# Banded attention with top-1 experts on one core: a block's transposes of p in one run, 64-row transposes of x, one-hot rows first in a step, one ring of eight PSUM banks

## The chip, the cores and the metric

The kernel runs on one core of one Trainium2 chip. The metric is the device time of one execution in microseconds (us): the median of three runs before the change is 515.14 us (509.45 to 516.59). The profiled execution of the same kernel took 514.24 us, of which the profile's span covers 512.5 us.

## What is computed

Four batches of eight heads attend over 768 positions with 64 values each; a query sees 8 global keys and the 95 positions before it, with a slope per head for the distance. The 3072 rows of the result (512 wide) go through a gate that picks one of eight experts for each row; an expert takes the first 768 rows that chose it.

```python
scores = scale * np.matmul(q, k.transpose(0, 1, 3, 2))
scores = scores + bias[None, :, :, :]
scores = np.where(keep, scores, -1000000000.0)
a = np.exp(scores - np.max(scores, axis=-1, keepdims=True))
a = a / (np.sum(a, axis=-1, keepdims=True) + 1e-09)
x = np.matmul(a, v).transpose(0, 2, 1, 3).reshape(B * S, H * D)
...
logits = x @ w_gate
expert_idx = np.argmax(logits, axis=1)
probs = softmax(logits)
# row i is row pos[i] of its expert, as long as pos[i] < 768
h = np.maximum(np.einsum('ecd,edf->ecf', disp, w1), 0.0)
y = np.einsum('ecf,efd->ecd', h, w2)
out[i] = gate_w[i] * y[expert_idx[i], pos[i]]
```

## The kernel before, in words

**Stages.** Attention runs over 24 blocks of 128 rows (4 batches of 6 blocks) in a loop of 25 steps, t = 0 to 24. The experts' products follow; the change leaves them alone.

**One step.** A block has two units of four heads. Step t scores block t, finishes block t-1 and passes block t-2 on: `scores` (PE, L516, 16 matmuls a unit), `maxima` (DVE, L492, four a unit: adds the bias and takes the row's extreme), `exps` (ACT, L527, four a unit, which also give the row sums), `transpose_p` (PE L554, 16 transposes a unit into two banks, copied out by DVE L555 and ACT L556; a batch's first block has four transposes and one copy, L545 and L546), `weigh` (PE L575 and L578: x^T from p and v), `keep_x` (ACT L585: x^T out of PSUM), `sums` and `turn_sums` (POOL L531, DVE L536: one over the row sums) and `store_rows` (PE L165: four 128x128 transposes of x^T, DVE L168: scaled rows, then a store by SP).

**The gate.** Blocks go through the gate in groups of three, in steps of `route`: z (PE L186, ACT L189), l (PE L196, DVE L198 and L202), m (DVE L208 and L215, POOL L216 and L217), f (DVE L222 and L225 make `oh`, the one-hot rows; POOL L224 zeroes its last columns), n (PE L231 and L233 count with `oh`), p and s (slots), g (DVE L273) and the writes (POOL, three indirect DMAs to a table, L283). With b a group's last block, z stands in step b+2, l and m in b+3, f, n, p and s in b+4, and g with the writes in b+5. So steps repeat in threes: a z-step (t = 4, 7, 10, ...; the writes of the group before fall in it too), an l-step (5, 8, 11, ...) and an n-step (6, 9, 12, ...).

**What sets the order.** The order on PE, DVE, ACT and POOL is the order in which this loop is written; only SP's DMAs are scheduled. Transposes for a block's second unit stand in the middle of the next step, those for its first unit at the end of its own step (L554 for unit 2t). From t = 9 to 20 a step ends with a piece of the first experts' weights (ACT cast L137, POOL subtraction L138).

**PSUM.** Eight banks in three pools: four bankA (scores, x rows, l, n), two bankB (p transposed), two bankC (x^T and z).

Of the kernel before, what the change touches and what calls it, by code (L numbers as in the profile page):

```python
# [10 lines left out]
F32 = mybir.dt.float32  # L11
# [6 lines left out]
ALU = mybir.AluOpType  # L18
# [11 lines left out]
def fused(ctx: ExitStack, tc, q, k, v, wg, w1, w2, out, shape, n_global, n_local, cap):  # L30
# [19 lines left out]
    psA = ctx.enter_context(tc.tile_pool(name="psA", bufs=4, space=bass.MemoryType.PSUM))  # L50
    psB = ctx.enter_context(tc.tile_pool(name="psB", bufs=2, space=bass.MemoryType.PSUM))
    psC = ctx.enter_context(tc.tile_pool(name="psC", bufs=2, space=bass.MemoryType.PSUM))
# [5 lines left out]
    def bankA(shape, dt=F32):  # L58
        return psA.tile(shape, dt, name="bankA")

    def bankB(shape, dt=F32):
        return psB.tile(shape, dt, name="bankB")

    def bankC(shape, dt=F32):
        return psC.tile(shape, dt, name="bankC")
# [7 lines left out]
    warm_ps = bankB([P, DM])  # L73
# [76 lines left out]
    actx = ExitStack()  # L150
# [10 lines left out]
    def store_rows(i):  # L161
        xt = xts[i // 3]
        xr_ps = bankA([P, DM])
        for c in range(KC):
            nc.tensor.transpose(xr_ps[:, c * P:(c + 1) * P], xt[:, c, i % 3, :], ident)  # L165

        xr = rt.tile([P, DM], F32, name="xr_last", bufs=1) if i == NBLK - 1 else small.tile([P, DM], F32, name="xr")
        nc.vector.tensor_tensor(xr.rearrange("p (h d) -> p h d", h=H), xr_ps.rearrange("p (h d) -> p h d", h=H),  # L168
                                rss[i // 3][:, i % 3, :].unsqueeze(2).to_broadcast([P, H, D]), op=ALU.mult)
        nc.sync.dma_start(out=xrows[i * P:(i + 1) * P, :], in_=xr)  # L170
# [8 lines left out]
    def route_z(r):  # L179
        i0, T = r["i0"], r["T"]  # L180
        bank = bankC([P, 4 * P])
        r["bank"] = bankA if i0 + T < NBLK else lambda shape: bank[:, 2 * P:2 * P + shape[1]]
        z_ps = bank[:, 0:T * P]
# [158 lines left out]
    def turn_first(a):  # L342

        ps = bankA([P, KC, P])
# [69 lines left out]
    def banded():  # L414
# [81 lines left out]
        def scores(u):  # L496
# [9 lines left out]
            pss = un["ps"] = [bankA([P, 2, w]) for _ in range(2)]  # L506
# [31 lines left out]
        def transpose_p(u):  # L538
            un = units[u]
            j = blocks[u // 2][1]  # L540
            pt = un["pt"] = soft.tile([P, 2, 4, P], F32, name="pt", bufs=3)
            if j == 0:
                pb = bankB([P, 4, P])
# [4 lines left out]
            pbs = [bankB([P, 2, 4, HQ]) for _ in range(2)]  # L548
            for a in range(4):
                for part in range(2):  # L550
                    for n in range(2):
                        rows = slice(n * HQ, (n + 1) * HQ)
                        o = a * W + (1 - n) * HQ + part * (PREV + G)
                        nc.tensor.transpose(pbs[n][:, part, a, :], un["flat"][rows, o:o + P], ident[rows, rows])  # L554
            nc.vector.tensor_copy(pt[:, :, :, 0:HQ], pbs[0])  # L555
            nc.scalar.copy(pt[:, :, :, HQ:], pbs[1])  # L556

        def weigh(u):
# [4 lines left out]
            if half == 0:  # L563
                d["xt_ps"] = bankC([P, KC, P])
# [36 lines left out]
        for t in range(NBLK + 1):  # L601
# [3 lines left out]
            if t < NBLK:  # L605
                for u in (2 * t, 2 * t + 1):
                    scores(u)
                    maxima(u)
                exps(2 * t)
            route(t - 3, 1)  # L610
            if t < NBLK:
                route(t - 4, 3)
                route(t - 5, 7, 8)
            if t > 0:
                sums(t - 1)
                transpose_p(2 * t - 1)
            if t == NBLK - 1:
# [5 lines left out]
            if t > 1:  # L623
                store_rows(x)
# [9 lines left out]
            if t < NBLK:  # L634
                if t < NBLK - 1:
                    route(t - 3, 2)
                route(t - 4, 6)
                exps(2 * t + 1)
                transpose_p(2 * t)
# [20 lines left out]
    def dense():  # L660
# [7 lines left out]
        for i in range(NBLK):  # L668
            b, j = divmod(i, NB)
            if j == 0:  # L670
                kt = kv.tile([P, NP, S], F32, name="kt")
                vt = kv.tile([P, NB, H * D], F32, name="vt")
                for jj in range(NB):
# [5 lines left out]
                    ps = bankC([P, NP, P])  # L679
# [6 lines left out]
            ps = bankC([P, NP, P])  # L686
# [25 lines left out]
            for h in range(H):  # L712
                g, rows = h // 2, slice(64 * (h % 2), 64 * (h % 2) + 64)
                sc = dn.tile([P, S], F32, name="sc")
                for c0 in range(0, S, 384):
                    c = slice(c0, min(c0 + 384, S))
                    s_ps = bankA([P, c.stop - c0])
# [12 lines left out]
                x_ps = bankB([P, P])  # L730
                for jj in range(NB):
                    pt_ps = bankC([P, P])
# [32 lines left out]
    actx.close()  # L765

# [126 lines left out]
    h_ps = [bankB([P, T4]) for _ in range(FP)]  # L893
    y_ps = [bankA([P, DM]) for _ in range(FIXED)]
# [292 lines left out]
```

## Time and profile before

| | before |
|---|---|
| median of 3 runs | 515.14 us |
| profiled execution | 514.24 us |
| its span | 512.5 us |
| PE busy | 458.4 us (89%) |
| DVE, ACT, POOL busy | 285.4, 284.5, 126.0 us |
| start of step 2, of step 23 | 15.33, 154.42 us |

A row of a timeline gives the start, the length, the engine, the line and the tiles (out<-in), how many instructions it joins, and, in brackets, how long the engine had been idle before it and what ended that. PE counts as busy while a matmul is in flight, at whatever clock was granted.

### The profile page before, as it was taken

How to read it: one execution, taken by the hardware profiler on the slowest of the kernel's cores; microseconds unless marked ns; L12 is line 12 of the kernel's file. 1: busy time of each engine (PE TensorE's matmuls, PEld its weight loads, DVE VectorE, ACT ScalarE, POOL GpSimd, SP SyncE). 2: the span in 40 equal slices, each digit the busy share in tenths (PEclk: the TensorE clock that was granted, in tenths of full speed). 3: DMA queues.
4: the chain of work that ended last, by engine and by line, in shares of the span. 5: the costliest groups of instructions: out<-in, count | busy, mean ns of one | idle time of the engine just before them, and what ended most of it. 6: DMA issues, size and time to landing. Idle time of an engine off the chain costs nothing.

```text
span 512.5 us, 11225 instructions
## 1 busy us (share of the span) xinstructions
PE 458.4 (89%) x3914; PEld 377.2 (74%) x3914; DVE 285.4 (56%) x920; ACT 284.5 (56%) x790; POOL 126.0 (25%) x208
## 2 busy tenths in 40 slices
PE   8998788888887759999999999999999999999860
PEld 4776667666675548788888888897988888897640
DVE  6776766668775732645554556545555555546320
ACT  4987777788784303345546546546555455546330
POOL 6022143453433230423113113113113103003020
PEclk9999898999997987999999999999999999999995
DMA  8999659967622076754465365365455445241010
GB/s 258 308 331 295 120 126 299 209 200 176 114 94 79 24 182 224 237 187 155 117 198 174 118 219 171 106 206 170 133 184 185 112 161 172 66 128 68 5 41 12
DMA packets 51782, 81.53 MB, mean 159 GB/s; under 512 B 7689, under 2 KB 20009, under 8 KB 51660
## 3 DMA queue, kind: packets, MB, share of 16 engines
q1 hardware_dynamic: 45084, 65.00, 43.9%
q0 software_dynamic: 5888, 14.71, 9.2%
q8 instruction: 92, 1.51, 1.2%
q14 instruction: 30, 0.25, 0.2%
q10 hardware_dynamic: 688, 0.07, 0.1%
HBM read 67.10 MB, written 14.75 MB: 160 GB/s over the span
## 4 chain that ended last, share of the span: by engine, by line
issue 59%; PE 14%; POOL 13%; ACT 4%; DVE 3%; DMA 3%; another core or an unknown queue 1%; POOLq 0%; SPq 0%; ACTq 0%
POOL xg L352 5%; POOL out_dram L825 4%; PE bankB L554 3%; PE bankC L575 3%; PE bankA L516 2%; PE bankC L578 2%; POOL table L283 2%; DVE sc L492 2%; PE bankA L165 2%; ACT sc L527 2%; ACT pt L556 1%; DMA table<-pay,slot_of 1%; DMA K<-in_k_dram 1%; DMA w2r<-in_moe_w_dram 1%
## 5 line engine op out<-in xcount | busy, mean ns | idle before, releaser
L916 PE MATMUL bankB<-xh,w1h 128*128 128x416 f32 (+5 forms) x268 | 90.0, 341 | 3.0 <-DVE hl L964 1.8
L916 PE MATMUL bankB<-xh,w1l 128*128 128x416 f32 (+5 forms) x268 | 88.8, 337 | 0.8 <-issue 0.8
L963 ACT ACTIVATE hh<-bankB 128x512 fp32r<-128x512 f32 (+1 forms) x67 | 38.8, 580 | 90.3 <-PE bankB L916 81.9
L527 ACT ACTIVATE sc<-sc,mx 128x168 f32<-128x168 f32 (+1 forms) x192 | 80.0, 422 | 6.9 <-DVE mx L492 6.6
L964 DVE SCALAR_TENSOR_TENSOR hl<-bankB,hh 128x512 fp32r<-128x512 f32 (+1 forms) x67 | 44.6, 666 | 69.9 <-ACT hh L963 66.2
L924 PE MATMUL bankA<-w2h,hh 128*128 128x512 f32 x192 | 80.8, 421 | 2.0 <-issue 1.9
L925 PE MATMUL bankA<-w2l,hh 128*128 128x512 f32 x192 | 76.9, 401 | 0.0
L926 PE MATMUL bankA<-w2h,hl 128*128 128x512 f32 x192 | 76.8, 400 | 0.0
L916 PEld LDWEIGHTS bankB<-xh,w1h 128*128 128x128 f32 x268 | 50.6, 189 | 11.4 <-issue 6.0
L352 POOL DMA_INDIRECT xg<-xrows,gi x28 | 28.5, 1017 | 118.8 <-PE bankC L337 103.2
L916 PE MATMUL bankB<-xl,w1h 128*128 128x416 f32 (+5 forms) x268 | 57.3, 336 | 0.0
L916 PEld LDWEIGHTS bankB<-xh,w1l 128*128 128x128 f32 x268 | 50.6, 189 | 3.9 <-issue 1.1
L138 DVE TENSOR_TENSOR w1l<-wr,w1h 128x512 fp32r<-128x512 f32 x58 | 37.5, 689 | 27.8 <-ACT w1h L137 22.1
L966 ACT ACTIVATE hr<-bankB 128x256 f32<-128x256 f32 x64 | 24.6, 385 | 49.5 <-DVE hl L964 44.2
L492 DVE CUSTOM_DVE_ANT_0 sc<-bankA,bias 128x168 f32<-128x168 f32 (+1 forms) x192 | 49.2, 321 | 2.2 <-PE bankA L516 1.5
L138 DVE TENSOR_TENSOR w2l<-w2r,w2h 128x512 fp32r<-128x512 f32 x58 | 37.5, 688 | 19.2 <-ACT w2h L137 18.2
L916 PEld LDWEIGHTS bankB<-xl,w1h 128*128 128x128 f32 x268 | 47.0, 188 | 0.6
L924 PEld LDWEIGHTS bankA<-w2h,hh 128*128 128x128 f32 x192 | 36.7, 191 | 13.9 <-issue 7.6
L825 POOL DMA_INDIRECT out_dram<-ysb,to x16 | 15.9, 997 | 126.3 <-ACT ysb L817 123.9
L516 PE MATMUL bankA<-K,Q 64*64 64x168 f32 (+1 forms) x704 | 41.1, 322 | 4.0 <-issue 2.7
L926 PEld LDWEIGHTS bankA<-w2h,hl 128*128 128x128 f32 x192 | 36.8, 191 | 8.9
L925 PEld LDWEIGHTS bankA<-w2l,hh 128*128 128x128 f32 x192 | 36.9, 192 | 5.8
(174 smaller groups left out, 745.7 us busy)
## 6 DMA issues: line engine op xcount, KB each, us to landing
wr<-in_moe_w_dram SPq DMA_DIRECT2D x58, 256.0 KB
w2r<-in_moe_w_dram SPq DMA_DIRECT2D x58, 256.0 KB
K<-in_k_dram SPq DMA_DIRECT2D x24, 272.0 KB
Q<-in_q_dram SPq DMA_DIRECT2D x24, 256.0 KB
v<-in_v_dram SPq DMA_DIRECT2D x24, 256.0 KB
xrows<-xr SPq DMA_DIRECT2D x23, 256.0 KB
v<-in_v_dram SPq DMA_DIRECT2D x20, 208.0 KB
wst<-in_moe_w_dram SPq DMA_DIRECT2D x12, 256.0 KB
```

The costliest lines, as they stand in the source:

```text
L138: (nc.gpsimd if meanwhile else nc.vector).tensor_tensor(parts["l"][:, s], r, parts["h"].bitcast(F32)[:, s], op=ALU.subtract)
L352: ld = nc.gpsimd.indirect_dma_start(out=xg, out_offset=None, in_=xrows[0:n], in_offset=bass.IndirectOffsetOnAxis(ap=gi.bitcast(U32), axis= ...
L492: nc.vector.tensor_tensor_reduce(out=un["sc"][:, a, HQ:HQ + un["w"]], in0=un["ps"][hh][:, gg, :], in1=un["bias"][:, 4 * (u % 2) + a, :], s ...
L516: nc.tensor.matmul(pss[hh][at, gg, :], d["qt"][rows, g, at], keys[b][rows, g, first_key:first_key + w], start=True, stop=True)
L527: un["e"] = nc.scalar.activation(sc[:, a, HQ:HQ + w], sc[:, a, HQ:HQ + w], AF.Exp, bias=un["mx"][:, a:a + 1], scale=-1.0, accum_out=sm[:, ...
L825: w = nc.gpsimd.indirect_dma_start(out=out, out_offset=bass.IndirectOffsetOnAxis(ap=rows.bitcast(U32)[:, 0:1], axis=0), in_=ysb, in_offset ...
L916: nc.tensor.matmul(h_ps[:, s], ww[:, c, fs], xx[:, c, s], start=n == 0, stop=n == 3 * KC - 1)
L924: nc.tensor.matmul(y, hh[:, t], w2h[:, fi], start=f == 0, stop=False)
L925: nc.tensor.matmul(y, hh[:, t], w2l[:, fi], start=False, stop=False)
L926: nc.tensor.matmul(y, hl[:, t], w2h[:, fi], start=False, stop=f == NF - 1)
L963: nc.scalar.activation(hh[:, s], h[:, s], AF.Relu)
L964: nc.vector.scalar_tensor_tensor(hl[:, s], h[:, s], 0.0, hh.bitcast(F32)[:, s], op0=ALU.max, op1=ALU.subtract)
```

## The change

Five edits, all in attention:

- The transposes of p of both units of block t-1 stand in one run after the scores of step t; the run at the end of a step is gone.
- `store_rows` turns x^T in eight transposes of 64 rows into two banks and scales it in two DVE operations of half the size.
- f stands first in a step, ahead of the maxima; n and l behind `store_rows`.
- g and the writes (three indirect DMAs on POOL) stand behind `weigh`, and so behind `sums`; they stood ahead of `sums` before.
- The three pools of PSUM banks become one ring of eight for attention; the experts open their own pools when it is closed.

```diff
-    psA = ctx.enter_context(tc.tile_pool(name="psA", bufs=4, space=bass.MemoryType.PSUM))
-    psB = ctx.enter_context(tc.tile_pool(name="psB", bufs=2, space=bass.MemoryType.PSUM))
-    psC = ctx.enter_context(tc.tile_pool(name="psC", bufs=2, space=bass.MemoryType.PSUM))
+    actx = ExitStack()
+    ring = actx.enter_context(tc.tile_pool(name="ring", bufs=8, space=bass.MemoryType.PSUM))
...
     def store_rows(i):
         xt = xts[i // 3]
-        xr_ps = bankA([P, DM])
+        xr_ps = [bank([P, KC, D]) for _ in range(2)]
         for c in range(KC):
-            nc.tensor.transpose(xr_ps[:, c * P:(c + 1) * P], xt[:, c, i % 3, :], ident)
+            for n in range(2):
+                rows = slice(n * D, (n + 1) * D)
+                nc.tensor.transpose(xr_ps[n][:, c, :], xt[rows, c, i % 3, :], ident[rows, rows])
...
-        nc.vector.tensor_tensor(xr.rearrange("p (h d) -> p h d", h=H), xr_ps.rearrange("p (h d) -> p h d", h=H),
-                                rss[i // 3][:, i % 3, :].unsqueeze(2).to_broadcast([P, H, D]), op=ALU.mult)
+        for n in range(2):
+            nc.vector.tensor_tensor(xr.rearrange("p (c n d) -> p c n d", n=2, d=D)[:, :, n], xr_ps[n],
+                                    rss[i // 3][:, i % 3, :].rearrange("p (c n) -> p c n", n=2)[:, :, n].unsqueeze(2)
+                                    .to_broadcast([P, KC, D]), op=ALU.mult)
...
             if t < NBLK:
+                route(t - 4, 3)
                 for u in (2 * t, 2 * t + 1):
                     scores(u)
                     maxima(u)
                 exps(2 * t)
-            route(t - 3, 1)
-            if t < NBLK:
-                route(t - 4, 3)
-                route(t - 5, 7, 8)
             if t > 0:
                 sums(t - 1)
+                transpose_p(2 * t - 2)
                 transpose_p(2 * t - 1)
+            if t > 1:
+                store_rows(x)
+            route(t - 3, 1)
...
             if t < NBLK - 1:
                 route(t - 4, 4, 5)
-            if t > 1:
-                store_rows(x)
...
                 route(t - 4, 6)
+                route(t - 5, 7, 8)
                 exps(2 * t + 1)
-                transpose_p(2 * t)
                 if t > 0:
                     keep_x(t - 1)
```

PE in an n-step, before: the transposes of a block's first unit (sc_126), which stand at the end of the step before, the scores, the transposes of its second unit (sc_127), the counts with `oh`, the rows of x and the first products with v.

```order
L554 MATMUL bankB<-ident,sc_126 128x64 x16
L516 MATMUL bankA<-K,Q 64x168 x16
L554 MATMUL bankB<-ident,sc_127 128x64 x16
L231 LDWEIGHTS tri_bf
L231 MATMUL bankA<-oh,tri_bf 128x32
...
L165 MATMUL bankA<-ident,xt 128x128 x4
L575 MATMUL bankC<-pt,v_1630 64x128 x2
L578 MATMUL bankC<-pt,v 64x128 x2
```

The same place after the change; the two units' p are sc_120 and sc_121.

```order
L512 MATMUL bank<-K,Q 64x168 x16
L550 MATMUL bank<-ident,sc_120 128x64 x16
L550 MATMUL bank<-ident,sc_121 128x64 x16
L159 MATMUL bank<-ident,xt 128x64 x8
L227 LDWEIGHTS tri_bf
L227 MATMUL bank<-oh,tri_bf 128x32
...
L571 MATMUL bank<-pt,v_1663 64x128 x2
L574 MATMUL bank<-pt,v 64x128 x2
```

Both units' transposes now stand between the scores and the products that need them in the same step; the counts stand behind the rows of x.

POOL at the end of an n-step and through the z-step and the l-step, before: the last slot operation, a weight piece, the writes, the sums of two steps with a piece between, and the gate's m.

```order
L269 TENSOR_SCALAR s_1728<-s_1728 128x3
L138 TENSOR_TENSOR w2l<-wst,w2h 128x512
L283 DMA table<-pay,slot_of 6144x2 x3
L531 TENSOR_SCALAR sm<-sm 128x8
L138 TENSOR_TENSOR w1l<-wst,w1h 128x512
L531 TENSOR_SCALAR sm<-sm 128x8
L216 TENSOR_TENSOR eq<-eq,erev 128x24
```

The same place after the change.

```order
L265 TENSOR_SCALAR s_1788<-s_1788 128x3
L131 TENSOR_TENSOR w2l<-wst,w2h 128x512
L527 TENSOR_SCALAR sm<-sm 128x8
L279 DMA table<-pay,slot_of 6144x2 x3
L131 TENSOR_TENSOR w1l<-wst,w1h 128x512
L527 TENSOR_SCALAR sm<-sm 128x8
L212 TENSOR_TENSOR eq<-eq,erev 128x24
```

The z-step's sums moved ahead of the three writes.

DVE from the l-step's m into the n-step, after the change (before, the two operations of f, L222 and L225, stood behind the eight maxima of the n-step).

```order
L551 COPY pt<-bank 128x8x64 x2
L163 TENSOR_TENSOR xr<-bank,rs 128x4x64 x2
L194 TENSOR_TENSOR lh<-bank,rs 128x3x8x8
L198 TENSOR_REDUCE lg<-lh 128x24
L532 RECIPROCAL rs<-sm 128x8
L204 TENSOR_REDUCE m<-lg 128x3
L211 TENSOR_TENSOR eq<-lg,m 128x24
L218 TENSOR_REDUCE f<-eq 128x3
L221 TENSOR_TENSOR oh<-eq,f 128x24
L488 ISA sc_122,mx<-bank,bias_119 128x168
```

f now stands between the l-step's `eq` and the n-step's first maximum (the last row, of eight).

## Rows read from the trace of the kernel before

**Rows 1.** Busy time of each engine by stretch of the span: the window in us, its length, then for PE, PEld, DVE, ACT and POOL the busy us and the instructions, then granted clock of PE as a share of full speed, DMA share, GB/s. Steps 2 to 7, steps 8 to 22, steps 23 and 24, and the experts.

```profile
15.33:49.33 34.00, 32.09 (x572) 25.75 (x568) 26.51 (x133) 29.24 (x113) 4.87 (x20) 1.00 1.06 318
49.33:154.42 105.09, 89.92 (x1466) 69.61 (x1463) 72.84 (x371) 81.07 (x307) 40.52 (x73) 0.97 0.69 169
154.42:172.06 17.64, 13.40 (x176) 10.58 (x172) 10.20 (x46) 7.85 (x25) 4.59 (x8) 0.81 0.22 62
200.00:512.50 312.50, 290.76 (x1497) 247.32 (x1496) 155.24 (x260) 153.64 (x302) 60.13 (x60) 0.98 0.45 142
```

**Rows 2.** Groups of instructions by line from 15 to 155 us: busy us, mean ns of one, idle us of the engine just before them and what ended it. From the tables of PE, DVE and ACT.

```profile
L231 PE MATMUL bankA<-oh,tri_bf 128*128 128x32 bf16 x6 | 1.1, 183 | 8.8 <-POOL oh L224 3.3 <-DVE oh L225 2.8 <-POOL base L248 2.7
```

```profile
L536 DVE RECIPROCAL rs<-sm 128x8 f32<-128x8 f32 x20 | 3.9, 195 | 15.5 <-POOL sm L531 15.5
```

```profile
L556 ACT COPY pt<-bankB 128x512 f32<-128x512 f32 x36 | 20.8, 578 | 22.2 <-PE bankB L554 11.5 <-remote 10.7
```

**Rows 3.** Timeline of the l-step t = 14 (it begins at 92.82 us) and the end of the z-step before it.

```profile
91.25 1.08 POOL L283 DMA_INDIRECT table<-pay,slot_of  x1 [2.12 <-DVE pay L273]
...
92.19 0.71 PE L554 MATMUL bankB<-ident,sc 64*128 64x64 f32 x16
...
92.82 1.69 PE L516 MATMUL bankA<-K,Q 64*64 64x168 f32 x21
...
93.90 0.97 POOL L283 DMA_INDIRECT table<-pay,slot_of  x1 [0.30 <-issue]
...
94.94 0.23 POOL L531 TENSOR_SCALAR sm<-sm 128x8 f32<-128x8 f32 x1
95.20 0.20 DVE L536 RECIPROCAL rs<-sm 128x8 f32<-128x8 f32 x1 [3.06 <-POOL sm L531]
95.47 0.55 PE L516 MATMUL bankA<-K,Q 64*64 64x168 f32 x6 [0.20 <-issue]
...
95.62 0.59 ACT L556 COPY pt<-bankB 128x512 f32<-128x512 f32 x1 [2.22 <-remote]
```

**Rows 4.** Timeline around the start of the l-step t = 5, in which no write runs.

```profile
31.57 0.71 PE L554 MATMUL bankB<-ident,sc 64*128 64x64 f32 x16
...
32.40 0.59 ACT L556 COPY pt<-bankB 128x512 f32<-128x512 f32 x1 [0.45 <-PE bankB L554]
```

**Rows 5.** Timeline of PE in the z-step t = 10, which waits for nothing.

```profile
66.13 1.37 PE L516 MATMUL bankA<-K,Q 64*64 64x168 f32 x32
67.44 0.71 PE L554 MATMUL bankB<-ident,sc 64*128 64x64 f32 x16
68.08 0.66 PE L165 MATMUL bankA<-ident,xt 128*128 128x128 f32 x4
68.66 0.85 PE L186 MATMUL bankC<-xt,wg_sb 128*32 128x384 f32 x8
69.45 0.44 PE L575 MATMUL bankC<-pt,v 104*64 104x128 f32 x4
...
71.04 0.39 PE L578 MATMUL bankC<-pt,v 128*64 128x128 f32 x4
71.36 0.72 PE L554 MATMUL bankB<-ident,sc 64*128 64x64 f32 x16
```

**Rows 6.** Timeline of step t = 2, whose scores begin at 15.33 us: the first maximum, and the copies of its second unit's p, which wait for nothing but their engines' earlier work.

```profile
16.18 0.33 DVE L492 CUSTOM_DVE_ANT_0 sc<-bankA,bias 128x168 f32<-128x168 f32 x1
...
18.21 0.69 DVE L555 COPY pt<-bankB 128x512 f32<-128x512 f32 x1
...
18.31 0.56 ACT L556 COPY pt<-bankB 128x512 f32<-128x512 f32 x1
```

**Rows 7.** Timeline from the l-step t = 14 into the n-step t = 15 (which begins at 101.48 us): DVE and POOL on the gate, and PE behind its wait.

```profile
98.16 0.52 DVE L198 TENSOR_TENSOR lh<-bankA,rs 128x192 f32<-128x192 f32 x1
...
98.98 0.68 DVE L555 COPY pt<-bankB 128x512 f32<-128x512 f32 x1
...
100.17 0.20 DVE L536 RECIPROCAL rs<-sm 128x8 f32<-128x8 f32 x1
...
100.44 0.18 DVE L215 TENSOR_TENSOR eq<-lg,m 128x24 f32<-128x24 f32 x1
```

```profile
100.71 0.24 POOL L216 TENSOR_TENSOR eq<-eq,erev 128x24 f32<-128x24 f32 x1 [1.82 <-DVE eq L215]
```

```profile
104.36 0.17 DVE L222 TENSOR_REDUCE f<-eq 128x3 f32<-128x24 f32 x1
104.57 0.18 DVE L225 TENSOR_TENSOR oh<-eq,f 128x24 bf16<-128x24 f32 x1
```

```profile
104.89 0.18 PE L231 MATMUL bankA<-oh,tri_bf 128*128 128x32 bf16 x1 [1.40 <-DVE oh L225]
...
105.58 0.44 PE L575 MATMUL bankC<-pt,v 104*64 104x128 f32 x4
```

**Rows 8.** Busy time by stretch again (columns as in the first group): the two stretches of steps 2 to 22 at a low granted clock.

```profile
53.70:57.50 3.80, 3.80 (x35) 3.18 (x37) 3.49 (x17) 3.41 (x15) 0.03 (x1) 0.56 0.77 38
84.80:88.30 3.50, 3.50 (x36) 2.77 (x36) 1.10 (x5) 1.71 (x6) 0.69 (x2) 0.51 1.14 302
```

**Rows 9.** Timeline of PE in step 23: the products with v, from their first row to what follows them.

```profile
162.57 0.70 PE L575 MATMUL bankC<-pt,v 104*64 104x128 f32 x4
...
166.19 0.94 PE L554 MATMUL bankB<-ident,sc 64*128 64x64 f32 x16
```

More of the change, by code (lines that the diff above doesn't have):

```diff
@@ L56, in fused, with bank @@
     table = dram.tile([E * R, 2], F32, name="table")
[L58 to L65, printed above, removed]
+    def bank(shape, dt=F32):
+        return ring.tile(shape, dt, name="bank")
     SYNC = mybir.DependencyInfo(mybir.DependencyClass.Sync, mybir.DependencyReason.DATA)
@@ L72, in fused @@
     nc.vector.memset(warm, 1.0)
-    warm_ps = bankB([P, DM])
+    warm_ps = bank([P, DM])
     def busy(n):
@@ L180, in route_z @@
         i0, T = r["i0"], r["T"]
-        bank = bankC([P, 4 * P])
-        r["bank"] = bankA if i0 + T < NBLK else lambda shape: bank[:, 2 * P:2 * P + shape[1]]
-        z_ps = bank[:, 0:T * P]
+        zb = bank([P, 4 * P])
+        r["bank"] = bank if i0 + T < NBLK else lambda shape: zb[:, 2 * P:2 * P + shape[1]]
+        z_ps = zb[:, 0:T * P]
         xt = xts[i0 // 3][:, :, i0 % 3:i0 % 3 + T, :]
@@ L342, in turn_first @@
     def turn_first(a):
-        ps = bankA([P, KC, P])
+        ps = bank([P, KC, P])
         turn_rows(ps, first["rows"][a])
@@ L505, in scores @@
             un["mx"] = small.tile([P, 4], F32, name="mx", bufs=3)
-            pss = un["ps"] = [bankA([P, 2, w]) for _ in range(2)]
+            pss = un["ps"] = [bank([P, 2, w]) for _ in range(2)]
             for gg in range(2):
@@ L542, in transpose_p @@
             if j == 0:
-                pb = bankB([P, 4, P])
+                pb = bank([P, 4, P])
                 for a in range(4):
@@ L547, in transpose_p @@
                 return
-            pbs = [bankB([P, 2, 4, HQ]) for _ in range(2)]
+            pbs = [bank([P, 2, 4, HQ]) for _ in range(2)]
             for a in range(4):
@@ L563, in weigh @@
             if half == 0:
-                d["xt_ps"] = bankC([P, KC, P])
+                d["xt_ps"] = bank([P, KC, P])
             xt_ps = d["xt_ps"][:, 2 * half:2 * half + 2]
@@ L678, in dense @@
                                       in_=v[b, :, r, :].rearrange("h p d -> p h d"))
-                    ps = bankC([P, NP, P])
+                    ps = bank([P, NP, P])
                     for g in range(NP):
@@ L685, in dense @@
                               in_=q[b, :, j * P:(j + 1) * P, :].rearrange("h p d -> p h d"))
-            ps = bankC([P, NP, P])
+            ps = bank([P, NP, P])
             for g in range(NP):
@@ L716, in dense @@
                     c = slice(c0, min(c0 + 384, S))
-                    s_ps = bankA([P, c.stop - c0])
+                    s_ps = bank([P, c.stop - c0])
                     nc.tensor.matmul(s_ps, qt[rows, g, :], kt[rows, g, c], start=True, stop=True)
@@ L729, in dense @@
                 nc.vector.reciprocal(rss[i // 3][:, i % 3, h:h + 1], sm)
-                x_ps = bankB([P, P])
+                x_ps = bank([P, P])
                 for jj in range(NB):
-                    pt_ps = bankC([P, P])
+                    pt_ps = bank([P, P])
                     nc.tensor.transpose(pt_ps, sc[:, jj * P:(jj + 1) * P], ident)
@@ L765, in fused, with bankC @@
     actx.close()
+    psA = ctx.enter_context(tc.tile_pool(name="psA", bufs=FIXED, space=bass.MemoryType.PSUM))
+    psB = ctx.enter_context(tc.tile_pool(name="psB", bufs=FP, space=bass.MemoryType.PSUM))
+    psC = ctx.enter_context(tc.tile_pool(name="psC", bufs=2, space=bass.MemoryType.PSUM))
+    def bankC(shape, dt=F32):
+        return psC.tile(shape, dt, name="bankC")
     mctx = ExitStack()
@@ L890, in load_arm @@
         arms[e] = nc.values_load(arm[0:1, e:e + 1], engines=[PE], min_val=0, max_val=NV - 1)
-    h_ps = [bankB([P, T4]) for _ in range(FP)]
-    y_ps = [bankA([P, DM]) for _ in range(FIXED)]
+    h_ps = [psB.tile([P, T4], F32, name="bankB") for _ in range(FP)]
+    y_ps = [psA.tile([P, DM], F32, name="bankA") for _ in range(FIXED)]
     def widths(e):
```

1 line of the change is left out of this document (removed).

## The prediction

> **What bounds the kernel now.** I read the windows by stage first [rows 1]. The experts take 312.5 us, PE is busy for 290.8 of them, and the change leaves their code alone: no gain there. Steps 2 to 22 take 154.42 - 15.33 = 139.1 us, 6.62 a step. In steps 2 to 7 PE is busy 32.1 of 34.0 us: PE bounds them. In steps 8 to 22 it is busy 89.9 of 105.1, DVE 72.8, ACT 81.1, POOL 40.5: nothing is full, so waits decide. Per step of that stretch ACT works 81.07/15 = 5.40 us and DVE 4.86, which is a floor for any faster step. Then I read the idle time by line [rows 2]. The counts of the gate, which need the one-hot rows, keep PE idle 8.8 us in six steps; DVE's reciprocal of the sums waits 15.5 us for POOL; ACT's copies of p wait 10.7 us for something that the profile calls remote.
>
> The last two fall into the l-steps, so I read one [rows 3]. Three indirect writes run on POOL from 91.25 to 94.87 us; the sums are queued behind them (94.94), DVE's reciprocal behind the sums (95.20), and on DVE the copy of p and all eight maxima behind that. So the sums look like the cause. But ACT's copy, which waits for no sum, starts at 95.62 too, though the transposes that it copies ended at 92.90. In the l-step without writes [rows 4] the transposes end at 32.28 and ACT copies at 32.40. And PE's own issue limps meanwhile: 21 scores, then groups of six [rows 3]. So while the second and third write run, PE issues slowly and its completions reach the other engines late, until some 0.65 us after the third write ends. That is a reading of this trace, not a known rule, and the whole forecast turns on it.
>
> **The change part by part.**
>
> *Transposes in one run, 64-row turns of x (a gain on PE, small).* A step's PE work from a z-step without waits [rows 5]: scores 1.31, a unit's transposes 0.64, x rows 0.58, z 0.79, products 71.36 - 69.45 = 1.91 to the next transposes. The eight new turns move as many columns in all as eight of L554's sixteen, so I estimate 0.32 for 0.58 (bounds: 0.58, no gain, and 0.26, pure half). PE's sum in a z-step becomes 1.31 + 1.28 + 0.32 + 0.79 + 1.91 = 5.61, in the other steps about 5.0. Within the products a group of four follows the last at (71.04 - 69.45)/7 = 0.23, yet the first transpose follows the last group by 0.32 [rows 5]: about 0.1 for a change of form, and the run has some two changes less per step. The Trainium skill's "TensorEngine Tiling (Array Packing)", Key Properties, says that a change of tiling mode drains TensorE; the 0.1 us agrees, and by it alone the change would bring 21 x 0.2 = 4 us. I leave that out of the sum, because the next part, not PE's work, sets the step.
>
> *The same edit makes a loop (a cost).* Before, the first unit's transposes ran a step ahead of their products. Now all copies of p come after the maxima on DVE and after four exps on ACT. From the scores' start (15.33) [rows 1, 6] the first maximum comes at +0.85, DVE's copy at +2.88 to +3.57, ACT's at +2.98 to +3.54. A DVE result reaches PE 0.14 us after its end (104.75 to 104.89) [rows 7]. Products then start at +3.71 and last 1.91 [rows 5]: a step cannot be under 5.62 us, whichever kind it is, just at PE's 5.61 in a z-step and over ACT's 5.40. Behind the waiting products stand only the next scores. The second unit's copies (about 0.6 later on either engine) are covered by the first half of the products, 0.95 us. 21 x 5.62 = 118.0. Three steps score a batch's first block (half the scores, 0.33 sooner) and three weigh one (half of the products, 0.95 less, of which ACT's floor lets me count 0.85): -3.5, so 114.5.
>
> *One-hot rows first (the wait goes to DVE).* PE's wait of 1.4 us [rows 7] goes. But the rows of DVE now read: l-step's second copy 0.6, two scalings of half the size (0.4 each, an estimate between half of 0.68 and all of it), lh and lg 98.98 - 98.16 = 0.82, reciprocal and m 0.27, eq 0.18, over to POOL and back 100.95 - 100.62 = 0.33, f and oh 0.39 [rows 7]: 3.4 us after the first copy's end, while the next scores start 2.05 after it. So oh is done 1.35 us into the n-step, and maxima that could start at +0.85 start 0.5 late (bounds 0.2 and 1.1, with scalings at half or full price and a longer way over POOL). Six n-steps: +3.0, so 117.5. The memset of oh's last columns on POOL stands behind a weight piece; its reader on PE stands at about +2.9, so it is mostly hidden.
>
> *Writes behind the sums (a gain, and the open price).* DVE's 15.5 us at the sums [rows 2] go: the z-step's sums come before the writes, and the l-step's are ready, after writes and a weight piece, before DVE asks. The three writes then start when pay is there, near the end of the z-step: they ran from 1.57 us before the l-step's scores to 2.05 after [rows 3]; now I work out about -0.2 to +3.4, completions late until about +4.05. Normally the l-step's maxima would start at +0.85 and its copies at +2.88. If only the transposes' completions are late, copies slip by 1.2 us; if all scores' are, by 3.2; if the lateness hangs on something else, by 0. With PE's issue also slow from the second write on, I take 1.8 for each of five l-steps (8, 11, 14, 17, 20): +9.0, so 126.5.
>
> *The ring costs nothing.* A step asks for 11 or 12 banks; the bank asked for eight requests back has been copied out by then: scores' by maxima, p's by the copies that the products waited for, x^T's by keep_x, which ends about 0.8 into the next step while its bank is wanted at 1.9. Were keep_x late, its 0.59 would show. SP's DMAs keep their places; the store of x goes when the second scaling is done.
>
> *Clock.* Two stretches run at a granted clock of 0.56 and 0.51 [rows 8], the 1.2 GHz level, and lose 3.8 x 0.44 + 3.5 x 0.49 = 3.4 us. I keep that (0 to five such stretches): 126.5 + 3.4 = 129.9, against 139.1: -9.2.
>
> *The end.* Step 23 waits for one-hot rows too; PE idles 17.64 - 13.40 = 4.2 us there [rows 1]. I take -1.5 (0 to -4.2).
>
> Sum: 514.24 - 9.2 - 1.5 = 503.5, made against the profiled execution, which stands 0.2% under the median of 515.14.
>
> **The rivals.**
>
> *B, the late completions fall away* (they hung on the sums' chain, or on where the writes fell): no 9.0, and one slow stretch less. 503.5 - 9.0 - 1.7 = 493. For it: DVE's wait looks like the cause. Against: ACT's copy [rows 3], which waits for nothing of it.
>
> *C, the gain is given back*: late by 3.2 rather than 1.8 in five l-steps (+7.0), and each such gap costs a slow stretch of 1.7 us (five instead of two, +5.1): 515.6, no measurable change. For it: the l-step has no work that could fill PE's gap now; before, transposes lay there.
>
> *D, slower*: in every step PE runs out of work before the products (1.31 + 1.28 + 0.32 = 2.9 of 3.71 us), and the clock falls in them. At a low clock products took 166.19 - 162.57 = 3.62 us instead of 1.91 [rows 5, 9]: +1.7 a step, with the loop through the products. It decides from 7 of 21 steps on (503.5 + 12 = 515) and gives 527 at 14. Against it: after an idle 1.40 us the products of t = 15 went at full pitch [rows 7]. The Trainium skill's "TensorE: Matmul & The Clock Gate", in "Why this matters for your kernels", warns that idle gaps between bursts bring back the half-rate clock; by that page D is the danger of this change, and this trace shows two such stretches in 21 steps.
>
> **How the numbers follow.** A, the sum above: 0.50, with its own range 498 to 510 (lateness 0.8 to 3.2 a step). B 0.17, C 0.20, D 0.13. Some 2%, about what a measurement of this kernel can tell from no change, is 10.3 us: faster is under 504.8. A lies under it a little more than half of the time (0.27), all of B does, giving 0.45 with C's fast tail left out; the rest of A and C are the same (0.42); D is slower (0.13). The range takes in B's upper half and C: 490 to 517.
>
> **What would show it.** Right: no wait of 3 us at DVE's reciprocal; the counts on PE without a wait; scores starting every 5.6 us in steps 2 to 7 and in z-steps; ACT's and DVE's copies in l-steps late behind the third write; 7 to 8 us an l-step. Wrong: l-steps as short as the others (B), products at twice their length (D), copies of p waiting for maxima far beyond +2.9 in plain steps, or a wait of the scores for a bank of the ring. A step in which PE never waits before the products would show the loop mis-sized. If the profile's steps 2 to 22 total over 139 us, the cause stands in the loop or the clock; if under 121, the lateness was not tied to the writes.

## The result and the profile after

The changed kernel takes 493.37 us (median of four runs, 490.81 to 498.86) against 515.19 us: a ratio of 0.958, 95% interval 0.948 to 0.968. It is faster, by nearly twice what was forecast (21.8 us for 11.6); the time is that of rival B (493 us). Medians here and below take in every run, while ratios leave out runs over 1.5% above the fastest of their kernel. The profiled execution took 494.78 us, its span 492.9.

Windows by stage of the changed kernel, columns as in [rows 1]: steps 2 to 7, steps 8 to 22, step 23 and 24, the experts; and last a stretch inside step 15.

```profile
13.17:48.10 34.93, 30.34 (x593) 24.94 (x591) 26.34 (x139) 29.02 (x115) 4.09 (x19) 1.00 1.07 311
48.10:137.64 89.54, 79.34 (x1526) 65.47 (x1524) 73.72 (x389) 80.45 (x308) 40.15 (x73) 0.98 0.86 205
137.64:155.40 17.76, 12.57 (x211) 10.35 (x209) 11.02 (x51) 9.46 (x31) 8.30 (x11) 0.90 0.25 77
...
180.00:492.90 312.90, 291.00 (x1496) 246.69 (x1494) 155.25 (x260) 153.56 (x302) 60.18 (x60) 0.98 0.45 142
```

```profile
94.50:98.20 3.70, 3.51 (x33) 3.32 (x34) 2.36 (x12) 2.34 (x11) 0.46 (x2) 0.54 1.05 376
```

Steps 8 to 22 take 89.5 instead of 105.1 us, with nearly the same work on DVE, ACT and POOL: waits went, not work. Step 2 begins 2.2 us earlier (13.17 for 15.33), steps 2 to 7 are 0.9 longer, and from the scores of step 23 to the end of the span it is 355.3 instead of 358.1. In sum -2.16 + 0.93 - 15.55 - 2.82 = -19.6, the difference of the spans.

The l-steps carry it. From first score to first score they took 10.07, 7.58, 8.66, 7.42 and 8.66 us (steps 8, 11, 14, 17, 20), now 5.59, 5.61, 6.33, 5.58 and 6.10: 42.4 to 29.2 us, 13.2 of the 15.55. The timeline of the l-step t = 8, the counterpart of [rows 3]:

```profile
48.10 1.37 PE L512 MATMUL bank<-K,Q 64*64 64x168 f32 x32
...
48.58 1.20 POOL L279 DMA_INDIRECT table<-pay,slot_of  x1 [4.58 <-DVE pay L269]
...
48.95 0.33 DVE L488 CUSTOM_DVE_ANT_0 sc<-bank,bias 128x168 f32<-128x168 f32 x1 [0.68 <-PE bank L512]
...
49.40 1.21 PE L550 MATMUL bank<-ident,sc 64*128 64x64 f32 x32
...
50.98 1.28 DVE L551 COPY pt<-bank 128x512 f32<-128x512 f32 x2
51.15 1.05 ACT L552 COPY pt<-bank 128x512 f32<-128x512 f32 x2
51.37 0.97 POOL L279 DMA_INDIRECT table<-pay,slot_of  x1 [0.30 <-issue]
51.77 0.44 PE L571 MATMUL bank<-pt,v 104*64 104x128 f32 x4 [0.30 <-ACT pt L552]
...
52.41 0.23 POOL L527 TENSOR_SCALAR sm<-sm 128x8 f32<-128x8 f32 x1
...
53.66 0.19 DVE L532 RECIPROCAL rs<-sm 128x8 f32<-128x8 f32 x1
```

Three writes run from 48.58 to 52.34, and nothing waits for them: the first maximum comes 0.85 us after the scores' start, the copies at +2.88 and +3.05, the products at +3.67, the next scores at +5.59. That is the loop of the forecast, and PE issues its 32 scores and 32 transposes without a gap. The sums (52.41) still stand behind the writes, but DVE asks for them only at 53.66. The lateness that the forecast had charged to these five steps is not there. Steps 14 and 20 are longer for other reasons. In step 20 the products wait 0.81 us for ACT's copy of p, which stands behind the exps of the short step before (4.80 us) and a cast of weights. In step 14 the first maximum comes at +1.64, behind scaled rows of x that DVE began after 1.46 us of idling; with three buffers for these rows (a_xr3_again, below) DVE does not idle there.

New waits of DVE from 12 to 150 us (waiting line, what it waited for, us in all, times, longest):

```profile
DVE xr L163 <- DMA xrows<-xr: 5.4, 2, 3.6
...
DVE f L218 <- POOL eq L212: 2.1, 6, 0.4
```

The first row is the main loss: DVE may not overwrite the scaled rows of x (two buffers) before their store has read them. It makes two steps long, t = 5 (7.52 us) and t = 15 (10.37 us). DVE's part of the second:

```profile
88.20 0.76 DVE L163 TENSOR_TENSOR xr<-bank,rs 128x256 f32<-128x256 f32 x2 [1.80 <-DMA xrows<-xr]
...
90.02 0.18 DVE L211 TENSOR_TENSOR eq<-lg,m 128x24 f32<-128x24 f32 x1
...
90.55 0.18 DVE L218 TENSOR_REDUCE f<-eq 128x3 f32<-128x24 f32 x1 [0.35 <-POOL eq L212]
90.76 1.20 DVE L221 TENSOR_TENSOR oh<-eq,f 128x24 bf16<-128x24 f32 x1
91.89 0.32 DVE L488 CUSTOM_DVE_ANT_0 sc<-bank,bias 128x168 f32<-128x168 f32 x1
```

And PE's:

```profile
87.82 1.37 PE L512 MATMUL bank<-K,Q 64*64 64x168 f32 x32
...
92.86 0.68 PE L159 MATMUL bank<-ident,xt 64*128 64x64 f32 x8 [2.53 <-DVE mx L488]
...
94.69 0.69 PE L571 MATMUL bank<-pt,v 104*64 104x128 f32 x4 [0.57 <-ACT pt L552]
...
98.19 1.37 PE L512 MATMUL bank<-K,Q 64*64 64x168 f32 x32
```

The late store (1.80) delays the gate's chain, the one-hot rows stand behind it and ahead of the maxima and take 1.20 us for 0.18, so the first maximum comes 4.1 us into the step instead of 0.85; PE idles, and its products then run at a granted clock of 0.54, the 1.2 GHz level, 98.19 - 94.69 = 3.50 us instead of 1.9.

### The profile page after: what moved, and what is told of

The parts are those of the page before. It is cut to its first block, busy times and chain, and to the rows that moved or that the text cites. A ratio compares the mean times of both kernels' runs of the same rounds, so it can differ in the third digit from the quotient of the medians.

```text
span 492.9 us, 11548 instructions
## 1 busy us (share of the span) xinstructions
PE 438.5 (89%) x4010; PEld 366.7 (74%) x4010; DVE 285.7 (58%) x944; ACT 283.5 (58%) x790; POOL 126.1 (26%) x208
## 4 chain that ended last, share of the span: by engine, by line
PE 45%; issue 28%; ACT 7%; DMA 6%; DVE 5%; POOL 5%; SPq 1%; POOLq 0%; ACTq 0%; DVEq 0%
PE bankB L917 15%; PE bankA L925 5%; PE bankA L926 5%; PE bankA L927 5%; ACT sc L523 4%; PE bank L512 3%; PE bank L574 3%; PE bank L571 3%; DVE sc L488 2%; POOL out_dram L826 2%; PE bank L550 2%; ACT pt L552 2%; POOL xg L348 1%; PE bankC L333 1%; DMA Q<-in_q_dram 1%
## 5 line engine op out<-in xcount | busy, mean ns | idle before, releaser
L488 DVE CUSTOM_DVE_ANT_0 sc<-bank,bias 128x168 f32<-128x168 f32 (+1 forms) x192 | 49.0, 320 | 14.5 <-PE bank L512 14.5
L571 PE MATMUL bank<-pt,v 104*64 104x128 f32 x320 | 34.4, 287 | 8.1 <-ACT pt L552 7.2
```

Source lines behind the costliest of these rows:

```text
L488: nc.vector.tensor_tensor_reduce(out=un["sc"][:, a, HQ:HQ + un["w"]], in0=un["ps"][hh][:, gg, :], in1=un["bias"][:, 4 * (u % 2) + a, :], s ...
L571: nc.tensor.matmul(o_ap, d["v1"][:, h * D:(h + 1) * D], un["pt"][0:PREV + G, 0, a, :], start=True, stop=False)
```

## The experiments

The question: before the change, two things held an l-step [rows 3]. The sums stand behind the writes and DVE's reciprocal behind the sums; and PE's completions come late ("the hold" below) while the writes run. They ended within 0.3 us of each other, so the trace could not tell which one mattered. Theory L took the hold, theory S the sums.

What was measured, in one table. The steps are worked out from the starts of the scores in each trace; "8 to 22" is from the first score of step 8 to that of step 23. Each ratio is against runs of the kernel before that were made beside it: their medians are 517.35 us for the first four rows below "changed", then 513.28 (a_pad to a_oh_late), 512.39 (a_again to a_t_split) and 512.78 (the last two).

| run | us (median) | against before, 95% | steps 8 to 22 | l-steps 8, 11, 14, 17, 20 |
|---|---|---|---|---|
| before | 515.19 | | 105.1 | 10.1, 7.6, 8.7, 7.4, 8.7 |
| changed | 493.37 | 0.958 (0.948 to 0.968) | 89.5 | 5.6, 5.6, 6.3, 5.6, 6.1 |
| b_sums_first | 519.93 | 0.994 (0.987 to 1.001) | 110.9 | 10.1, 8.2, 10.2, 8.7, 10.2 |
| b_writes_last | 521.29 | 1.009 (1.004 to 1.014) | 108.2 | 8.7, 8.5, 10.7, 8.5, 11.5 |
| a_writes_early | 499.57 | 0.966 (0.961 to 0.970) | 94.3 | 7.6, 8.4, 7.7, 7.4, 7.6 |
| a_xr3 | 510.40 | 0.986 (0.982 to 0.990) | 104.4 | 10.4, 9.6, 10.0, 9.7, 10.5 |
| a_pad | 495.05 | 0.966 (0.958 to 0.974) | 89.0 | 5.6, 5.6, 6.1, 5.6, 6.1 |
| a_xr3_in_place | 491.86 | 0.959 (0.952 to 0.966) | 86.0 | 5.6, 5.6, 6.1, 5.6, 6.1 |
| a_oh_late | 495.44 | 0.963 (0.952 to 0.973) | 88.7 | 5.6, 5.6, 7.0, 5.6, 6.1 |
| a_again | 494.88 | 0.965 (0.957 to 0.972) | 89.1 | 5.6, 5.6, 6.1, 5.6, 6.1 |
| a_xr3_again | 489.72 | (two runs, 485.6 and 493.8) | 85.4 | 5.6, 5.6, 6.1, 5.6, 6.1 |
| a_t_split | 492.87 | 0.960 (0.952 to 0.968) | 91.6 | 5.4, 5.6, 5.9, 5.6, 5.9 |
| b_writes_last_again | 499.83 | 0.971 (0.963 to 0.979) | 92.6 | 6.2, 6.1, 6.2, 6.1, 6.2 |
| a_writes_early_again | 499.28 | 0.970 (0.964 to 0.977) | 95.6 | 8.8, 6.3, 8.6, 6.5, 8.9 |

Each of these four groups ran one run after another on one chip: the first two on the same one, the third and the fourth on two others. This matters below.

**The sums ahead of the writes.**

```diff
                 route(t - 4, 3)
-                route(t - 5, 7, 8)
             if t > 0:
                 sums(t - 1)
+            if t < NBLK:
+                route(t - 5, 7, 8)
+            if t > 0:
                 transpose_p(2 * t - 1)
```

> The kernel before, with one edit: the sums of a step stand ahead of the three indirect writes on POOL, the writes keep their place otherwise. Theory L (the one of the prediction: PE's completions reach the other engines late while the second and third write run): DVE's 3 us wait for the sums in l-steps goes, but ACT's copy of p still comes some 2.5 us after the transposes end, l-steps stay at 8 to 9 us and the time at 510 to 516 us. Theory S (the sums queued behind the writes were the whole cost, and what looked like late completions followed from it): copies come within 0.2 us of the transposes, l-steps fall by 2 to 3 us each, the time to 500 to 505 us.

Timeline around the l-step t = 14 of this run (an execution of 520.2 us):

```profile
92.53 0.19 DVE L536 RECIPROCAL rs<-sm 128x8 f32<-128x8 f32 x1
...
92.65 0.71 PE L554 MATMUL bankB<-ident,sc 64*128 64x64 f32 x16
93.10 0.97 POOL L283 DMA_INDIRECT table<-pay,slot_of  x1 [0.30 <-issue]
...
94.37 0.97 POOL L283 DMA_INDIRECT table<-pay,slot_of  x1 [0.30 <-issue]
94.54 0.54 PE L516 MATMUL bankA<-K,Q 64*64 64x168 f32 x4 [0.23 <-issue]
...
96.11 0.69 DVE L555 COPY pt<-bankB 128x512 f32<-128x512 f32 x1 [3.39 <-remote]
96.20 0.58 ACT L556 COPY pt<-bankB 128x512 f32<-128x512 f32 x1 [2.33 <-remote]
```

The reciprocal waits no more (92.53), yet DVE's copy of p waits 3.39 us: the transposes ended at 93.36, PE issues in groups of four to six, and both copies start 0.8 us after the third write's end. So the hold is real and needs no late sums. This went as theory L said, with l-steps of 8.2 to 10.2 us for its 8 to 9.

**The writes behind the products, in the kernel before.**

```diff
                 route(t - 4, 3)
-                route(t - 5, 7, 8)
...
                 route(t - 4, 6)
+                route(t - 5, 7, 8)
                 exps(2 * t + 1)
```

> The kernel before, with one edit: the reciprocal of pay and the three indirect writes stand behind the products with v, as in the changed kernel; nothing else is changed. Theory L: the writes start later, so the lateness falls about 1.4 us later into the l-step and delays the maxima or the copies there by 1 to 3 us; l-steps 7 to 8 us, 506 to 513 us. Theory S: the sums come ahead of the writes, l-steps fall to 6 us, 500 to 504 us. Theory P (it is not the order against the sums but which PE work runs beside the writes that counts: scores beside the second and third write are late, transposes and products are not): l-steps at 6 to 6.5 us, and no late completion, since the second write now starts when the scores are nearly issued.

It came out no faster, 1.009, with holds in all five l-steps, of 8.5 to 11.5 us: theory L has such holds, but shorter steps (7 to 8 us) and a gain, and S and P have none.

**The writes back at their old place, in the changed kernel.** The same lines the other way round: behind the first exps and ahead of the sums.

> The changed kernel, with one edit: the reciprocal of pay and the three indirect writes stand again where the kernel before has them, behind the first four exps and ahead of the sums. Theory L: late completions again; the writes run beside the products of the z-step and the next scores, l-steps 7 to 8 us instead of 5.6, 500 to 505 us. Theory S: DVE's reciprocal of the sums waits 2 to 3 us at the end of each z-step with writes and delays the next maxima by about 1 us; copies of p on ACT are not late against the transposes; 495 to 499 us.

499.57 us, between the two; the trace had both the wait for the sums and PE's gaps.

**Three buffers for the scaled rows of x.**

```diff
-        xr = rt.tile([P, DM], F32, name="xr_last", bufs=1) if i == NBLK - 1 else small.tile([P, DM], F32, name="xr")
+        xr = rt.tile([P, DM], F32, name="xr_last", bufs=1) if i == NBLK - 1 else small.tile([P, DM], F32, name="xr", bufs=3)
```

> The changed kernel, with one edit: the scaled rows of x (xr) have three buffers instead of two, so that DVE need not wait until the store of two blocks before has left its buffer. If that wait made steps 5, 14 and 15 long (7.5, 6.3 and 10.4 us against 5.6), they fall to 5.6 to 6.2 and the time by 4 to 7 us, to 486 to 489 us. Rival: the stores are late because the DMA queues are full of loads, and the backlog then shows as later Q, K and v: the steps stay long, 491 to 495 us.

This fitted neither side: 510 us. Order on all engines is the same as in the changed kernel; DVE's waits for stores are gone, the addresses of what stands behind xr in SBUF have moved by 2 KB. Yet every l-step shows the hold. Timeline of step 8:

```profile
46.86 1.37 PE L512 MATMUL bank<-K,Q 64*64 64x168 f32 x32
...
47.33 1.20 POOL L279 DMA_INDIRECT table<-pay,slot_of  x1 [4.58 <-DVE pay L269]
...
48.16 0.82 PE L550 MATMUL bank<-ident,sc 64*128 64x64 f32 x18
...
49.44 0.26 PE L550 MATMUL bank<-ident,sc 64*128 64x64 f32 x1 [0.47 <-issue]
...
50.12 0.97 POOL L279 DMA_INDIRECT table<-pay,slot_of  x1 [0.30 <-issue]
50.17 0.31 PE L550 MATMUL bank<-ident,sc 64*128 64x64 f32 x3 [0.48 <-issue]
...
51.85 0.33 DVE L488 CUSTOM_DVE_ANT_0 sc<-bank,bias 128x168 f32<-128x168 f32 x1 [2.83 <-remote]
```

Writes, scores and transposes stand as in step 8 of the changed kernel, to 0.1 us from the scores' start; but PE's issue stops at the 18th transpose, and DVE's fifth maximum, whose scores were issued by 48.23, waits 2.83 us. And in each of the five l-steps PE comes to a stretch at the 1.2 GHz level behind the hold (windows, columns as in [rows 1]):

```profile
51.20:58.00 6.80, 6.30 (x65) 5.28 (x64) 4.48 (x19) 3.33 (x11) 1.09 (x6) 0.50 0.73 122
75.10:78.50 3.40, 3.40 (x34) 3.07 (x30) 2.48 (x10) 1.18 (x7) 0.42 (x2) 0.50 0.77 125
95.60:98.90 3.30, 3.30 (x37) 2.94 (x37) 2.26 (x10) 1.02 (x5) 0.42 (x2) 0.50 0.68 138
116.10:119.40 3.30, 3.30 (x32) 3.15 (x31) 2.30 (x8) 1.22 (x6) 0.15 (x1) 0.50 0.61 63
136.60:139.90 3.30, 3.30 (x32) 3.20 (x32) 2.60 (x10) 0.82 (x4) 0.42 (x2) 0.50 0.77 90
```

Two more kernels tell addresses from waits.

**Addresses alone, and waits alone.** The first makes a small tile 2 KB larger, so that addresses are those of the 510 us run; the second has three buffers, with that small tile (`slot_i`) in a pool of its own at the end of SBUF, so that addresses are those of the changed kernel.

```diff
-        slot_i = small.tile([P, T4], I32, name="slot_i", bufs=1)
+        slot_i = small.tile([P, 2 * T4], I32, name="slot_i", bufs=1)[:, 0:T4]
```

> The changed kernel, with one edit: a small tile of slot numbers is made 2 KB a partition larger, so that all tiles behind it (Q, K, v, p, the scores, the weights) stand at the addresses of the run with three buffers of xr, while order and waits are those of the changed kernel. Theory M (where tiles stand in SBUF decides whether PE's completions are held while the three writes run): the hold is back in all l-steps, 9.5 to 10.5 us each, 505 to 512 us. Theory D (the waits of DVE for stores of x, and with them the phase of loads and stores, decide): l-steps at 5.6 to 6.3 us as in the changed kernel, 490 to 498 us.

```diff
-        xr = rt.tile([P, DM], F32, name="xr_last", bufs=1) if i == NBLK - 1 else small.tile([P, DM], F32, name="xr")
+        xr = rt.tile([P, DM], F32, name="xr_last", bufs=1) if i == NBLK - 1 else small.tile([P, DM], F32, name="xr", bufs=3)
...
-        slot_i = small.tile([P, T4], I32, name="slot_i", bufs=1)
+        slot_i = last_pool[0].tile([P, T4], I32, name="slot_i", bufs=1)
...
+        last_pool.append(actx.enter_context(tc.tile_pool(name="lastp", bufs=1)))
```

> The changed kernel with three buffers of xr, and the slot numbers moved to the end of SBUF in exchange, so that every other tile keeps its address. Theory M: no hold, and steps 5, 14 and 15 (7.5, 6.3 and 10.4 us in the changed kernel) at about 6: 484 to 490 us. Theory D: holds as with three buffers before, l-steps of about 10 us, 505 to 512 us.

Neither brought the hold back: 495 and 492 us. Both theories fell, each on its own run. What was left: both together, or something outside the program.

**The same kernels again.**

> The changed kernel once more, unedited, beside the next two on one chip. If it is a property of the program that PE's completions are not held in its l-steps, they take 5.6 to 6.3 us again and the time is 490 to 498 us. If the hold comes and goes with the loading of a program, some l-steps may show 7 to 10 us, 498 to 512 us.

> The changed kernel with three buffers of xr once more, unedited: neither the addresses alone nor the missing waits alone brought its 510 us back. If the hold is a property of this program, l-steps of about 10 us and 508 to 514 us again. If it came with that one loading, l-steps of 5.6 to 6.3 us and 488 to 494 us.

The changed kernel took 494.9 us again, but the 510 us kernel 485.6 and 493.8. The same place of it, step 8:

```profile
46.59 1.37 PE L512 MATMUL bank<-K,Q 64*64 64x168 f32 x32
...
47.07 1.20 POOL L279 DMA_INDIRECT table<-pay,slot_of  x1 [4.57 <-DVE pay L269]
...
47.89 1.21 PE L550 MATMUL bank<-ident,sc 64*128 64x64 f32 x32
...
49.47 1.28 DVE L551 COPY pt<-bank 128x512 f32<-128x512 f32 x2
```

One program, the writes at the same place to 0.01 us: no hold. All four traces of the first group have it beside the writes, none of the later ones of the changed kernel or its variants. So the program alone doesn't decide it. Nor does the chip alone: the second group ran free of it where the first had it. But no kernel with the hold was run a second time on the same chip, so a chip's part in it is not ruled out. And the first three experiments had all been read with the hold there. What they said of the sums was open again; the two that decide were repeated.

> The kernel before with the writes behind the products once more, unedited: its first run fell into the call in which even the changed kernel with three buffers of xr showed holds, so it may have been that call. If the writes' place (behind sums and products) is what keeps PE's completions from being held, l-steps are 6 to 6.6 us now and the time 498 to 504 us. If it takes the changed order on PE or DVE as well, holds as before: l-steps of 8.5 us and more, 513 to 522 us.

499.83 us, 0.971 (0.963 to 0.979): without the hold the one move of the writes gives the kernel before l-steps of 6.1 to 6.2 us, and takes off 512.8 - 499.8 = 13.0 us (the median of before beside it was 512.78) of the 21.8 that the whole change brings. DVE's list of waits has none for the sums any more. The runs of before beside it were not traced, so it is not shown that they too were free of the hold, and that all of the 13.0 is the sums'.

> The changed kernel with the writes at their old place once more, unedited, for the same reason. If the writes' place decides, the hold is there again: l-steps 7.4 to 8.4 us, 497 to 502 us. If the first call made the holds, l-steps are 5.6 to 6.5 us (DVE's wait for the sums adds up to 1 us to the next maxima), 490 to 497 us.

499.28 us, as before, but for another reason than the hold: no gaps in PE's issue, and instead

```profile
DVE rs L532 <- POOL sm L527: 12.2, 5, 2.6
```

in the waits of DVE: the sums again stand behind the writes, and the maxima of five l-steps behind the reciprocal. So neither reading of the expectation fits: the time is that of the first, the steps show no hold. Without the hold theory S holds, and its price is 12.2 us of DVE's time and some 5 us of the whole. In three of these l-steps (8, 14, 20: 8.6 to 8.9 us) PE's granted clock falls to 0.50, the 1.2 GHz level, after its wait for the maxima, so the price is the wait and the clock together.

**One-hot rows behind the maxima, in the changed kernel.**

```diff
-                route(t - 4, 3)
                 for u in (2 * t, 2 * t + 1):
                     scores(u)
                     maxima(u)
                 exps(2 * t)
+                route(t - 4, 3)
```

> The changed kernel, with one edit: the one-hot rows are made behind the eight maxima again, as in the kernel before. By the prediction's terms the n-steps trade 0.5 us at the start of the maxima for 0.4 us between maxima and copies of p, and PE's counts wait for the one-hot rows until about 3.4 us into the step, ahead of products that could start at 3.7: no change beyond 2 us, 491 to 496 us. If one-hot rows first is what took PE's wait away, n-steps grow by 1 us or more, 499 to 503 us.

495.44 us, interval 0.952 to 0.973: no difference that shows.

**The first unit's transposes at the end of their step again, in the changed kernel.**

```diff
-                transpose_p(2 * t - 2)
                 transpose_p(2 * t - 1)
...
                 exps(2 * t + 1)
+                transpose_p(2 * t)
```

> The changed kernel, with one edit: the transposes of p of a block's first unit stand at the end of their own step again, those of its second unit in the next step, as in the kernel before; writes, one-hot rows, 64-row turns and the ring stay changed. Theory O (the order of PE's transposes, scores and products beside the writes decides on the hold): holds as in the kernel before with writes last, l-steps 8.5 to 10 us, 505 to 515 us. Theory W (the place of the writes and of the one-hot rows decides): l-steps under 6.5 us; a step has no loop from its own scores to its products for half of them, so steps 2 to 7 stay at 5.4 to 6.0 us, 490 to 497 us.

492.87 us, interval 0.952 to 0.968: no difference either. Steps 2 and 3 take 5.38 us, 0.2 less than with all transposes in one run.

With the writes moved the kernel before takes 499.8 us, with the whole change 493.4. These 6.4 us were found in no single part: the one-hot rows and the transposes can each go back without a loss that shows, and the 64-row turns and the ring were not tested alone.

## Why the prediction was right or wrong

*The direction was right, the size about half.* The forecast was 503.5 us, the median 493.4, inside the range only because that took in rival B. The step that failed is the term of 9.0 us "completions late" in five l-steps (1.8 each): that the hold goes with the writes wherever they stand. It measured 29.2 - 5 x 5.58 = 1.3 us, and not as lateness: it is what steps 14 and 20 lost to ACT's copy and to the scaled rows of x. What the prediction read in [rows 3] was there: b_sums_first shows copies held with the sums long done. Wrong was to take it for a property of the writes, which moves with them. It had been present in the one trace that there was; the trace of the changed kernel had none, and a_xr3 against a_xr3_again shows it come and go in one program. Where it came with the writes at their new place, in a_xr3, it made l-steps of 9.6 to 10.5 us, on average 4.5 over 5.58, with a stretch at a granted clock of 0.50 in each of the five, and 510.4 us: that is close to rival C (3.2 and a slow stretch of 1.7 a step, 515.6 us). So with the changed order the term was either near 0 or about 22 us, and 1.8 a step fits neither. That no hold fell on the runs of the changed kernel is luck, as far as the runs show.

Because before the change the sums' chain (DVE free at 95.40) and the hold (copies at 95.62) ended together [rows 3], a trace with the hold hid how much the sums alone cost. DVE's 15.5 us at the sums [rows 2], which the prediction set aside for the row of ACT's copy, are then the price that the changed order takes away. This follows from the two runs made again (13.0 and some 5 us) and not from a trace of the kernel before without the hold, of which there is none. Rival B had the time, 493, but not the reason: it hung the hold on the sums or on the writes' place, and b_sums_first has it without the one, a_xr3 with the writes at the new place. Nor had it the waits for the stores or the gains at start and end, so that its number came out so near is in part luck too.

*The loop was right.* 5.62 us forecast, 5.58 measured in five undisturbed steps (2, 3, 16, 17, 22); first maximum at +0.85, copies at +2.88, products at +3.67 for +3.71. A first block weighed gives 4.80 us (4.77 forecast). A first block scored gives 5.72, 5.59 and 5.61 us where 0.33 less was forecast: half the scores do not start the maxima sooner by enough to show.

*One-hot rows first* cost up to 0.6 us in n-steps, 0.5 forecast (t = 9: 6.09, t = 21: 6.20, t = 6: 5.72 us); PE's wait of 1.4 us went in steps 6 to 21 (the longest left is 0.33). Putting them back changed nothing that shows, so wait and delay about balance, as the expectation of that run had worked out.

*Transposes in one run* brought nothing that can be measured (a_t_split): plain steps are 0.2 us longer with them, so the loop, not PE's work, sets the step, as forecast. Two readings on the way there were slightly off, and nothing hangs on them: half of 0.58 us for the turns is 0.29, not 0.26, and behind the 21 scores of [rows 3] PE issues a group of five and one of six.

*Missed:* DVE's wait for the store of x. The prediction looked at the store's place in SP's queue, not at who waits for its end. 1.9 us in step 5 and 4.8 in step 15, the second with a stretch at the 1.2 GHz level. The forecast loss of 3.4 us in such stretches came to 3.50 - 1.91 = 1.6 in one, inside the 4.8. Three buffers take the wait away (a_xr3_again, a_xr3_in_place: step 15 in 5.58 and 6.25 us, steps 8 to 22 in 85.4 and 86.0), though step 5 stays at 6.87 us in the second, where PE halts 1.49 us on "issue"; but 489.7 and 491.9 us are not told apart from 493.4.

*Start and end* gave 2.2 and 2.8 us where 1.5 in all was in the sum. At the end the one-hot rows of step 23 are still waited for, 3.37 us; the start gains in step 0 and 1, which the prediction had not costed.

The sum with the measured terms: 503.5 - 9.0 + 1.3 (steps 14 and 20 in place of the lateness) - 3.4 + 1.9 + 4.8 (clock and stores) - 2.2 - 1.3 (start, rest of the end) = 495.6, against the profiled 494.8.

*Rival D* did not happen: in the l-step shown PE idles 0.30 us before the products and they run at full pitch (0.44 for the first four, as in [rows 5]); only after the halt in step 15, where the turns of x^T wait 2.53 us for the maxima, did the clock fall. The Trainium skill's "TensorE: Matmul & The Clock Gate" ("Why this matters for your kernels") warns of idle gaps between bursts; the trace agrees in one step of 21, with its 0.54 in step 15.

## What to carry to other kernels

When two waits end together, a trace shows the cost of neither; before charging one of them to the changed kernel, work out the time with each of them gone, and give the cases chances of similar weight. A short operation that another engine needs (the sums, 0.23 us) should not stand in a queue behind slow ones (three writes, 3.6 us); that one move was worth 13 us in the kernel before and some 5 in the changed one. A wait that comes and goes between runs of one program needs a second trace before any kernel is charged with it. And when a store's or a load's place is kept, still ask which engine waits for its end: DVE's waits for these stores were 1.4 us in all before the change and 5.4 after.

## What was not expected of the hardware

PE's hold: in some runs PE's issue limps (one to six matmuls at a time, 0.2 to 0.5 us apart, charged to "issue") and its completions reach DVE, ACT and the queues late, until 0.7 to 0.9 us after the last of three indirect writes on POOL; in other runs of the very same program, with the writes at the same place against the scores, nothing of it shows (510.4 and 489.7 us, five runs of 509.5 to 513.5 and two of 485.6 and 493.8). With the writes it stood in every l-step of a trace or in none. Shorter ones stood away from them: single halts on "issue" of 1.5 to 2.3 us in step 5 of a_xr3, a_oh_late and a_xr3_in_place, and a hold once each in step 9 of a_xr3_in_place, a_oh_late and a_t_split; timelines of PE and DVE in step 9 of a_xr3_in_place, whose last write ended at 53.38:

```profile
56.02 1.21 PE L550 MATMUL bank<-ident,sc 64*128 64x64 f32 x32
...
60.23 0.31 PE L574 MATMUL bank<-pt,v 128*64 128x128 f32 x1 [0.49 <-issue]
...
60.35 0.69 DVE L551 COPY pt<-bank 128x512 f32<-128x512 f32 x1 [1.77 <-remote]
```

The copy takes transposes that ended by 57.23, again with PE halting on "issue". So the writes are where it mostly falls, not shown to be its cause. What decides is open: addresses in SBUF, the waits for stores, the writes' place and the order on PE were each changed, none decides alone, and the chip was another one when the held kernels were run again; and the DMA queue that carries instructions shows a packet between 49.0 and 49.5 us in a_xr3 and in a_xr3_again alike. Whether the kernel before is free of it in some runs was not seen; its runs lay between 508 and 520 us throughout, which would fit if the sums hide it.

The one-hot operation in step 15 took 1.20 us instead of 0.18 (its median). POOL's subtraction of a weight piece ran at the same time (timeline of POOL in the changed kernel):

```profile
90.66 1.26 POOL L131 TENSOR_TENSOR w1l<-wst,w1h 128x512 fp32r<-128x512 f32 x1
```

The Trainium skill's "SBUF — State Buffer", "Who interferes with whom", says that a DVE operation with two inputs from SBUF contends with a GpSimd operation that reads SBUF, over a pair of ports that they share and that one at a time holds; this row agrees with it (the two end at 91.96 and 91.92), but no run here was made to show it.
